# A fused linear-attention and feed-forward kernel: the opening's order of work written anew up to chunk 3, and the last tile stored in three pieces

## The chip, the core and the metric

The kernel runs on one core of a Trainium2 chip. The metric is the device time of one execution in microseconds (us). A core has a matrix engine (TensorE, PE in the profile, with its weight loads shown as PEld), a vector engine (VectorE, DVE), a scalar engine (ScalarE, ACT), a general engine (GpSimd, POOL) and a sync engine (SyncE, SP) that here only issues transfers. Transfers (DMAs) are done by 16 DMA engines that all queues share. Each engine works through its own list of instructions strictly in order; waits between engines are semaphores. TensorE reads SBUF, the on-chip memory, and writes PSUM, eight accumulator banks.

## What is computed

Lightning attention over 4 sequences (b) of 768 positions with 8 heads of 64 columns, and on its output a feed-forward block with an activation that has one slope per hidden column:

```python
for b in range(nb):                       # blocks of positions
    intra = (q_b @ k_b.T * Dmask) @ v_b
    inter = (q_b * lam_pow) @ kv_state
    out_b = intra + inter
    kv_state = lam_block * kv_state + (k_b * rev_pow).T @ v_b
x = out.transpose(0, 2, 1, 3).reshape(3072, 512)
h = x @ w_in                              # 512 -> 2048
g = maximum(h, 0) + alpha * minimum(h, 0)
y = g @ w_out                             # 2048 -> 512
```

q, k, v, w_in and w_out lie in DRAM as 32-bit floats, 4 MB for each of w_in and w_out; the matrix products are done in 16-bit floats.

## The kernel before, in words

The 3072 rows are cut into 6 chunks c of 512 rows. A chunk holds two sequences (bi = 0, 1) of 256 positions each, and each of these two groups of four heads (hh = 0, 1): four *units* per chunk, numbered n = 4c + 2bi + hh, 24 in all.

For a chunk's data, `load(c, bi, x, half)` (L80) issues from SP the transfer of k, q or v of one sequence: 512 KB, or with half 0 or 1 the 256 KB of one head group. There are five sets of buffers for these (L49). SP's transfers use eight semaphores in turn, so that a transfer also waits until the one issued eight before it has landed. `load_win(i)` and `load_wout(i)` (L95, L101) issue from POOL a quarter of w_in or w_out, which is cast to 16 bits on the way (1 MB read, 512 KB written). `gate(i, which)` (L109) is a transfer of a single element out of a weight quarter, issued from SP: since SP works in order, every load that stands behind it in SP's list waits until that quarter has landed.

A unit goes through these steps. `cast` (L254) makes 16-bit copies of k, q and v on ACT ("A"), DVE ("V") or POOL ("G"). `key_decayed` (L267) is the decayed k for the state. `transposes` (L284) brings q and k into columns, either on PE with a copy out of PSUM by ACT or DVE, or ("D") as a DMA transpose from SP; `transposed` (L310) does q or k alone on PE. `decayed` (L328) is the decayed q. `cluster(old, new)` (L343) is the matrix work: for `new` the scores s (L375) and the state update (L402), for `old` the state's part (L358) and the product of masked scores and v (L387); behind it the mask on DVE (L413), the copy of the old unit's output to XT on ACT or DVE (L420), and the state's copies R and RD (L433 to L451).

`up(c, f, bi, bank)` (L456) is one of 16 column blocks of h for a chunk (four matmuls of 512 columns, or of 256 with bi given, which needs just that sequence's two units), with the activation on ACT (L469) and DVE (L478). `down(c, t, part, 4, bank)` (L485) is a quarter of the sum for one of a chunk's four output tiles (four matmuls); part p reads quarter p of w_out, and up(f) reads quarter f // 4 of w_in. The last part calls `store` (L502): a copy on ACT and a transfer from SP. `down_last` (L509) does the output tiles of the last chunk, which nothing is left to overlap with; the last of them is cut into two halves of 256 columns. `fill` (L130) issues matmuls whose result nobody reads.

The order of all this is written out: the calls from L561 to L770 stand in the order in which each engine gets its instructions, and take the kernel to the end of up(1). From there, the loop at L772 weaves up(c) and down(c - 1) with the attention of chunk c + 1, for c = 2 to 5, and L781 ends with the last chunk's tiles. In that opening list, chunk 0's loads come first; the POOL list has load_win(0) and (1) at L611, (2) and (3) at L635, the four quarters of w_out at L639 and L657. SP's list has chunk 1's first sequence ungated (L620 to L625), gate(0, "out") ahead of the second sequence's k and q (L645), and gate(2, "out") ahead of chunk 2 (L688). Before up(0) gets going at L632 the list has 27 matmuls of `fill` behind the four of L146.

Of the kernel before, what the change touches and what calls it, by code (L numbers as in the profile page):

```python
# [11 lines left out]
def kernel(  # L12
# [102 lines left out]
    def zero_states(batches):  # L115
        for b in batches:
            for hh in (1, 0):
                nc.vector.memset(RD[b, hh], 0.0)
# [390 lines left out]
    def down_last(c, t, nc_parts):  # L509
        n = DM // nc_parts  # L510
        for x in range(nc_parts):
            o_ps = h_ps_pool.tile([128, DM], fp32, tag="h", name="o_ps")
            for f in range(NF):
                nc.tensor.matmul(  # L514
                    o_ps[:, 0:n],
                    lhsT=lhs(c, f, t),
                    rhs=w_out_sb[:, f, ts(x, n)],
                    start=(f == 0),
                    stop=(f == NF - 1),
                )  # L520
            store(c, t, o_ps, x * n, n)
# [38 lines left out]

    query_decay(2, 1)  # L561
    query_decay(1, 1)
    mask_logs(2)
    load(0, 0, "k", 0)
    query_decay(0, 1)
    cast(0, "k16", "G")
    load(0, 0, "q", 0)
    load(0, 0, "v", 0)
    load(0, 0, "k", 1)
    mask_logs(0)  # L570
    cast(0, "q16", "V")
    key_decay()
    load(0, 0, "q", 1)
    cast(0, "v16", "A")
    mask_logs(1)
    decay_mask(1)
    mask_logs(3)
    decay_mask(3)
    key_decayed(0, "G")
    load(0, 0, "v", 1)  # L580
    fill(4, "h")
    transposes(0, "V", False)
    decayed(0, "V")
    query_decay(3, 1)
    cast(1, "k16", "G")
    state_decay()
    cast(1, "q16", "G")
    load(0, 1, "k", 0)
    load(0, 1, "q", 0)
    load(0, 1, "v", 0)  # L590
    load(0, 1, "k", 1)
    load(0, 1, "q", 1)
    decay_mask(0)
    fill(5, "h")
    cluster(None, 0)
    slopes()
    transposed(1, 1, "V", "tk")
    cast(1, "v16", "A")
    transposed(1, 0, "A", "h")
    decayed(1, "P")  # L600
    fill(3, "op")
    cluster(0, None, "V")
    cast(2, "q16", "A")
    decay_mask(2)
    key_decayed(1, "G")
    key_decayed(2, "V")
    cast(2, "v16", "A")
    cast(2, "k16", "G")
    cluster(None, 1)
    transposed(2, 0, "V", "h")  # L610
    load_win(0)  # L611
    load_win(1)
    cast(3, "q16", "G")
    cast(3, "k16", "A")
    transposed(2, 1, "A", "op")
    query_decay(1, 0)
    fill(5, "tk")
    transposed(3, 1, "V", "tk")
    load(0, 1, "v", 1)
    load(1, 0, "k", None)  # L620
    transposed(3, 0, "A", "h")
    decayed(2, "G")
    cluster(1, 2, "A")
    load(1, 0, "q", None)
    load(1, 0, "v", None)  # L625
    cast(3, "v16", "A")
    key_decayed(3, "G")
    decayed(3, "G")
    fill(7, "h")
    cluster(2, 3, "A")  # L630
    fill(3, "op")
    up(0, 2, 0, "h")  # L632
    up(0, 0, 0, "h")
    cluster(3, None, "A")
    load_win(2)  # L635
    load_win(3)
    up(0, 1, 0, "h")
    up(0, 1, 1, "h")
    load_wout(0)  # L639
    load_wout(1)  # L640
    zero_states((2, 3))
    up(0, 3, None, "tk")
    up(0, 6, None, "h")
    key_decayed(5, "G")
    gate(0, "out")  # L645
    up(0, 7, None, "op")
    up(0, 0, 1, "h")
    load(1, 1, "k", None)
    up(0, 5, None, "tk")
    up(0, 2, 1, "h")  # L650
    up(0, 11, None, "op")
    load(1, 1, "q", None)
    up(0, 4, None, "h")
    up(0, 8, None, "tk")
    up(0, 10, None, "op")
    cast(4, "k16", "A")
    load_wout(2)  # L657
    load_wout(3)
    up(0, 15, None, "h")
    query_decay(2, 0)  # L660
    up(0, 9, None, "h")
    cast(5, "k16", "G")
    up(0, 12, None, "op")
    key_decayed(4, "V")
    up(0, 13, None, "tk")
    cast(5, "q16", "G")
# [146 lines left out]
```

## Time and profile before

| | us |
|---|---|
| three runs: median | 219.85 |
| three runs: lowest to highest | 219.68 to 221.3 |
| profiled execution: span from the first to the last instruction | 218.5 |
| the median over that span | 1.35 more |

No time but its span is given for the profiled execution itself. The span is taken by the hardware profiler and leaves out what lies around the first and last instruction. In the rows, "x4" is a count of instructions, the first two numbers of a row in order of time are its start and its length in us, and what stands in brackets is how long the engine had been idle and who ended that. L87 is a line of the kernel before. A busy PE isn't PE at its peak: matmuls overlap, and one of 512 columns that follows another adds 0.22 us while its own duration is shown as 0.38 us.

### The profile page before, as it was taken

The numbers are of one execution on the slowest core, as the hardware profiler recorded it, in microseconds if no ns is written. First come the engines' busy times: TensorE is split into PE (matmuls) and PEld (weight loads), VectorE is DVE, ScalarE is ACT, GpSimd is POOL, SyncE is SP. The second block draws the span as 40 slices with busy tenths as digits, with TensorE's granted clock in tenths as the row PEclk, the third lists the DMA queues.
The fourth block names the chain that finished last, engine by engine and source line by source line (L and its number), as shares of the span: only waits on it lengthen the run. The fifth ranks groups of instructions, "written<-read, shape, count | busy, mean of one in ns | idle before, by whom it ended". The sixth has DMA issues, their size and how long they took to land.

```text
span 218.5 us, 5177 instructions
## 1 busy us (share of the span) xinstructions
PE 206.5 (94%) x2065; PEld 104.7 (48%) x2065; DVE 131.5 (60%) x261; ACT 112.5 (51%) x216; POOL 92.3 (42%) x165
## 2 busy tenths in 40 slices
PE   7788899988979999999999999999999999999993
PEld 2454445544445444555545545554545444444453
DVE  7986788467879964866855646546645444444000
ACT  6886577246555575365456445545445434444121
POOL 4779300265099873697693484375331000000000
PEclk9999999999999999999999999999999999999999
DMA  5999999995799999689757997232111011110212
GB/s 149 297 274 215 216 214 206 270 282 153 184 273 208 315 238 209 164 208 231 176 126 192 149 244 222 57 96 65 35 51 48 0 51 49 48 48 0 99 48 96
DMA packets 62332, 33.90 MB, mean 155 GB/s; under 512 B 18132, under 2 KB 59364, under 8 KB 62308
## 3 DMA queue, kind: packets, MB, share of 16 engines
q1 hardware_dynamic: 58036, 29.37, 54.3%
q0 software_dynamic: 4224, 4.19, 11.4%
q8 instruction: 16, 0.26, 0.6%
q14 instruction: 8, 0.07, 0.1%
q10 hardware_dynamic: 48, 0.01, 0.0%
HBM read 27.27 MB, written 6.29 MB: 154 GB/s over the span
## 4 chain that ended last, share of the span: by engine, by line
PE 77%; DMA 11%; POOL 3%; DVE 3%; issue 2%; SPq 1%; ACT 1%; ACTq 0%; DVEq 0%
PE h_ps L461 34%; PE o_ps L491 29%; PE o_ps L514 6%; DMA w_in_sb<-in_moe_w_in_dram 6%; PE s L375 3%; DMA kraw<-in_k_dram 3%; DMA qkT<-qk 3%; PE acc L387 2%; PE acc L358 2%; SPq L87 1%; PE acc L402 1%; POOL RD L451 1%; DVE xT L243 1%; DVE sm L413 1%; POOL qdT L333 1%
## 5 line engine op out<-in xcount | busy, mean ns | idle before, releaser
L478 DVE SCALAR_TENSOR_TENSOR g<-m,oma,h_ps 128x512 f16<-128x512 f32 (+1 forms) x100 | 71.3, 724 | 57.3 <-ACT m L469 56.3
L461 PE MATMUL h_ps<-xT,w_in_sb 128*128 128x512 f16 (+1 forms) x400 | 95.0, 371 | 1.4 <-DMA w_in_sb<-in_moe_w_in_dram 1.3
L469 ACT ACTIVATE m<-h_ps 128x512 f32<-128x512 f32 (+1 forms) x100 | 57.7, 579 | 64.4 <-PE h_ps L461 62.3
L491 PE MATMUL o_ps<-w_out_sb,g 128*128 128x512 f16 x320 | 81.3, 379 | 0.0
L461 PEld LDWEIGHTS <-w_in_sb 128*128 128x128 f16 x400 | 38.1, 98 | 44.5 <-DMA w_in_sb<-in_moe_w_in_dram 2.7
L491 PEld LDWEIGHTS <-g 128*128 128x128 f16 x320 | 30.1, 98 | 34.1
L413 DVE TENSOR_TENSOR sm<-s,dmask 128x512 f16<-128x512 f32 x48 | 30.8, 684 | 7.5 <-PE s L375 7.0
L451 POOL COPY RD<-R 64x128 f16<-64x128 f16 x64 | 18.5, 289 | 36.2 <-DVE R L437 34.3
L333 POOL TENSOR_TENSOR qdT<-qkT,qdecay 128x512 f16<-128x512 f16 (+1 forms) x21 | 22.0, 1049 | 20.7 <-DVE qkT L243 17.0
L271 POOL TENSOR_TENSOR kdec<-kraw,kdecay 128x512 f16<-128x512 f32 x22 | 23.0, 1045 | 1.8 <-ACT kdecay L210 1.8
L504 ACT ACTIVATE o_sb<-o_ps 128x512 f32<-128x512 f32 (+1 forms) x25 | 14.5, 580 | 17.0 <-PE o_ps L514 11.1
L245 POOL CAST qk<-kraw 128x512 f16<-128x512 f32 x19 | 11.6, 610 | 11.3 <-DMA kraw<-in_k_dram 10.6
L437 DVE SCALAR_TENSOR_TENSOR R<-R,rdecay,acc 128x64 f16<-128x64 f16 x64 | 14.2, 274 | 3.0 <-ACT R L434 3.0
L241 ACT ACTIVATE xT<-acc 128x512 f16<-128x512 f32 x18 | 10.7, 597 | 8.7 <-PE acc L402 7.7
L514 PE MATMUL o_ps<-w_out_sb,g 128*128 128x512 f16 (+1 forms) x80 | 14.0, 336 | 0.0
L375 PE MATMUL s<-qkT 64*64 64x128 f16 x384 | 10.0, 222 | 1.8 <-DMA qkT<-qk 1.1
L514 PEld LDWEIGHTS <-g 128*128 128x128 f16 x80 | 7.8, 98 | 6.3
L358 PE MATMUL acc<-qdT,RD 128*128 128x128 f16 x80 | 8.4, 219 | 2.5 <-DVE R L437 1.1
L358 PEld LDWEIGHTS <-RD 128*128 128x128 f16 x80 | 6.0, 97 | 9.1 <-ACT R L434 2.0
L241 ACT ACTIVATE qk<-qraw 128x512 f16<-128x512 f32 x15 | 9.3, 622 | 0.7 <-DMA qraw<-in_q_dram 0.7
L387 PE MATMUL acc<-sm,v 64*64 64x128 f16 x384 | 9.6, 218 | 0.0
L375 PEld LDWEIGHTS <-qkT 64*64 64x64 f16 x384 | 6.2, 106 | 6.1 <-DMA qkT<-qk 2.0
(62 smaller groups left out, 108.6 us busy)
## 6 DMA issues: line engine op xcount, KB each, us to landing
out_dram<-o_sb SPq DMA_DIRECT2D x23, 256.0 KB, 2.0
kraw<-in_k_dram SPq DMA_DIRECT2D x10, 512.0 KB, 6.1
qraw<-in_q_dram SPq DMA_DIRECT2D x10, 512.0 KB, 6.0
vraw<-in_v_dram SPq DMA_DIRECT2D x10, 512.0 KB, 5.2
w_in_sb<-in_moe_w_in_dram POOLq DMA_DIRECT2D x4, 512.0 KB, 11.6
w_out_sb<-in_moe_w_out_dram POOLq DMA_DIRECT2D x4, 512.0 KB, 18.2
kraw<-in_k_dram SPq DMA_DIRECT2D x4, 256.0 KB, 5.6
qraw<-in_q_dram SPq DMA_DIRECT2D x4, 256.0 KB, 5.4
```

Source lines behind the costliest of these rows:

```text
L241: nc.scalar.activation(out, in_, AF.Copy)
L271: engine(eng).tensor_tensor(out=kdec, in0=kr, in1=kdecay[:, ds(4 * hh, 4), :].rearrange("p h e -> p e h").unsqueeze(3).to_broadcast([128, ...
L333: engine(eng).tensor_tensor(out=qdT[:, :, :, p], in0=(t["qps"] if eng == "P" else t["qkT"][:, 0])[:, :, :, p], in1=qdecay[:, hh, :, :, p], ...
L358: nc.tensor.matmul(ot[a][:, hp, :].rearrange("p (e j) -> p e j", e=2), lhsT=RD[bb, ho][:, a, hp].rearrange("p h d -> p (h d)"), rhs=to["qd ...
L375: nc.tensor.matmul(s[hl][ds(a * 64, 64), hp, 1 - e, :].rearrange("p (e j) -> p e j", e=2), lhsT=t["qkT"][p, 1, e, hp, ds(a * 64, 64)], rhs ...
L413: nc.vector.tensor_tensor(out=sm, in0=s[hl], in1=mask_of(hl, hh), op=ALU.mult)
L451: nc.gpsimd.tensor_copy(out=RD[b, hh][p, a, :, hl, :], in_=R[b, hh, 2 * pb + a][p])
L461: nc.tensor.matmul(h_ps[:, 0:n] if bi is None else h_ps[:, 0:n].rearrange("p (e j) -> p e j", e=2), lhsT=w_in_sb[:, gi, ts(f, 128)], rhs=x ...
L469: nc.scalar.activation(m[:, 0:n], h_ps[:, 0:n], AF.Relu, scale=-1.0)
L478: nc.vector.scalar_tensor_tensor(out=g, in0=mv, scalar=oma[:, f : f + 1], in1=hv, op0=ALU.mult, op1=ALU.add)
L491: nc.tensor.matmul(o_ps, lhsT=lhs(c, f, t), rhs=w_out_sb[:, f, :], start=(f == 0), stop=(f == NF - 1),)
L514: nc.tensor.matmul(o_ps[:, 0:n], lhsT=lhs(c, f, t), rhs=w_out_sb[:, f, ts(x, n)], start=(f == 0), stop=(f == NF - 1),)
```

## The change

The written-out list is replaced by another that goes on to the end of up(2); the loop starts at c = 3. As far as the next sections use it:

- q of both sequences of chunk 0, and v of the second, are loaded whole; the order is k (second head group first), q, v.
- POOL gets load_win(0), (1), (2), (3) and load_wout(2) with at most two casts or products between any two of them, and load_wout(0), (1) right behind decayed(3).
- SP gets gate(2, "out") after chunk 0 and two 256 KB pieces of chunk 1 (k and q of unit 4). All the rest of chunk 1, in pieces of 256 KB, stands behind this gate. gate(1, "out") stands ahead of the last two of them and of chunk 2. load_wout(3) stands in POOL's list behind key_decayed(7), which needs a piece of chunk 1 that is loaded behind the gate.
- Unit 8 is transposed on PE in place of a DMA; 15 DMA transposes are left of 16. `fill` has 35 matmuls in place of 27, 17 of them before the first transpose.
- Chunk 1's attention is mixed with down(0), chunk 2's with up(1) and down(1), most of chunk 3's with down(1) and up(2).
- zero_states(2) goes to POOL, written as integers.
- The last tile is stored as 256, 128 and 128 columns in place of 256 and 256.

```diff
-    def down_last(c, t, nc_parts):
-        n = DM // nc_parts
-        for x in range(nc_parts):
+    def down_last(c, t, widths):
+        x = 0
+        for n in widths:
...
-        down_last(NC - 1, t, 1 if t < 3 else 2)
+        down_last(NC - 1, t, (DM,) if t < 3 else (256, 128, 128))
```

The new list up to the point at which up(1) begins:

```diff
+    query_decay(2, 0)
     query_decay(2, 1)
+    load(0, 0, "k", 1)
+    load(0, 0, "k", 0)
+    load(0, 0, "q", None)
     query_decay(1, 1)
+    fill(11, "h")
+    load(0, 0, "v", 0)
+    mask_logs(0)
     mask_logs(2)
+    fill(6, "h")
+    load(0, 0, "v", 1)
+    key_decay()
+    key_decayed(0, "G")
+    mask_logs(3)
+    load(0, 1, "k", 0)
+    cast(1, "k16", "G")
+    cast(0, "v16", "G")
+    decay_mask(0)
+    cast(0, "k16", "V")
+    mask_logs(1)
+    cast(2, "k16", "G")
+    key_decayed(1, "G")
+    load_win(0)
+    load(0, 1, "q", None)
+    cast(0, "q16", "V")
+    state_decay()
+    transposed(0, 1, "V", "op")
+    load(0, 1, "k", 1)
+    decay_mask(2)
+    transposed(0, 0, "V", "h")
+    transposed(1, 1, "V", "op")
     query_decay(0, 1)
+    load(0, 1, "v", None)
     decay_mask(1)
+    key_decayed(2, "G")
+    load(1, 0, "k", 0)
     decay_mask(3)
+    load_win(1)
     query_decay(3, 1)
+    decayed(0, "P")
+    cast(1, "q16", "A")
+    load_win(2)
+    cluster(None, 0)
     fill(5, "h")
+    transposed(1, 0, "A", "h")
+    cast(1, "v16", "A")
+    cast(3, "q16", "G")
+    transposed(2, 1, "V", "h")
+    decayed(1, "P")
+    load_win(3)
+    cast(2, "q16", "V")
+    load_wout(2)
+    cluster(0, 1, "A")
+    transposed(2, 0, "A", "tk")
+    cast(2, "v16", "V")
+    decayed(2, "V")
+    cast(4, "k16", "V")
+    fill(8, "h")
+    load(1, 0, "q", 0)
+    cluster(1, 2, "A")
+    cast(3, "k16", "A")
+    fill(5, "op")
+    cast(3, "v16", "G")
+    cast(4, "q16", "G")
+    transposed(3, 0, "V", "tk")
+    key_decayed(3, "V")
+    transposed(3, 1, "A", "h")
+    gate(2, "out")
+    cluster(2, None, "A")
+    load(1, 1, "k", 1)
+    key_decayed(4, "G")
+    cluster(None, 3, "A")
+    decayed(3, "G")
     slopes()
+    transposes(4, "A", False)
+    up(0, 1, 0, "h")
+    up(0, 3, 0, "op")
+    cluster(3, None, "A")
+    up(0, 2, 0, "h")
+    load(1, 0, "v", 0)
+    up(0, 2, 1, "h")
+    decayed(4, "V")
+    load(1, 0, "q", 1)
+    load_wout(0)
+    up(0, 0, None, "op")
+    up(0, 7, None, "tk")
+    up(0, 5, None, "h")
+    load_wout(1)
...
+    up(0, 1, 1, "tk")
+    load(1, 1, "k", 0)
+    down(0, 0, 0, 4, "op")
+    down(0, 2, 0, 4, "h")
+    down(0, 2, 1, 4, "h")
+    key_decayed(7, "G")
+    load_wout(3)
+    load(1, 1, "v", 0)
+    zero_states((3,), "V")
+    load(2, 0, "k", 0)
+    cast(4, "v16", "G")
+    key_decayed(5, "G")
+    cast(7, "q16", "A")
+    load(2, 0, "q", 0)
+    down(0, 3, 0, 4, "h")
+    cast(6, "k16", "G")
+    cast(5, "q16", "V")
+    cast(5, "k16", "V")
+    down(0, 3, 1, 4, "h")
+    cluster(None, 4)
+    transposes(5, "A", False)
...
+    down(0, 0, 1, 4, "op")
+    decayed(5, "V")
...
+    down(0, 2, 2, 4, "h")
...
+    cluster(4, 5, "A")
+    transposes(7, "A", False)
...
+    down(0, 0, 2, 4, "op")
+    cast(6, "q16", "A")
+    down(0, 3, 2, 4, "h")
+    cluster(5, 7, "A")
+    down(0, 0, 3, 4, "op")
...
+    transposes(6, "A", False)
...
+    cluster(7, 6, "A")
+    transposes(8, "A", False)
+    down(0, 1, 0, 4, "h")
...
+    down(0, 1, 1, 4, "h")
+    cluster(6, 8, "A")
...
+    down(0, 1, 2, 4, "h")
+    up(1, 4, None, "op")
...
+    cluster(15, 16, "A")
+    cast(17, "v16", "G")
+    up(2, 12, None, "tk")
+    cast(18, "v16", "G")
+    key_decayed(18, "G")
 
-    for c in range(2, NC):
+    for c in range(3, NC):
```

More of the change, by code (lines that the diff above doesn't have):

```diff
@@ L615 @@
-    transposed(2, 1, "A", "op")
-    query_decay(1, 0)
[L617 to L657, printed above, removed]
```

312 lines of the change are left out of this document (165 added, 147 removed).

## The prediction

> **What bounds the kernel now.** I read the page's busy shares first, then the busy time of each engine by stage, cut where the work changes.
>
> ```profile
> PE 206.5 (94%) x2065; PEld 104.7 (48%) x2065; DVE 131.5 (60%) x261; ACT 112.5 (51%) x216; POOL 92.3 (42%) x165
> ```
> ```profile
> 24.24:44.25 20.01, 20.01 (x142) 9.96 (x146) 14.15 (x24) 11.36 (x24) 2.32 (x4) 1.00 1.20 230
> 44.25:63.47 19.22, 16.09 (x296) 8.63 (x296) 14.28 (x33) 10.43 (x24) 9.22 (x13) 1.00 0.87 217
> 63.47:110.49 47.02, 46.84 (x556) 24.14 (x557) 36.36 (x76) 26.23 (x46) 34.75 (x65) 1.00 0.94 218
> 110.49:201.36 90.87, 90.87 (x714) 44.27 (x713) 47.23 (x77) 43.19 (x73) 29.02 (x55) 1.00 0.35 88
> ```
> Columns are stage, length, then busy us of PE, PEld, DVE, ACT, POOL, the granted clock, DMA share and GB/s. From 63 us on PE has practically no idle time, at full clock. 110.49 is where up(3, 0) starts, the first call that both versions' loop has in common (read by counting the steps in PE's order). From there on both lists are the same up to the last tile, and PE is full: 108.0 us of the span that the change can't shorten, save in the last tile. What is open is when up(3, 0) starts.
>
> How far that is from the least, I get by pricing PE's work in the full stretch. The chain of work gives the unit price.
>
> ```profile
> 37.49 0.45 PE tp L299 x8
> ...
> 41.55 2.59 PE o_ps L491 x12
> ...
> 57.17 5.71 DMA qkT<-qk
> ```
> Four matmuls of an up or a down cost 2.59/3 = 0.864 us. The stretch 110.49:201.36 holds ups and downs of three chunks, 96 x 0.864 = 82.9; the other 8.0 us are about eight clusters, so 1.0 us each (estimate; 0.88 for chunk 0 and 1, whose state part is half as large). A PE transpose of a unit costs 0.45.
>
> ```profile
> 20.02 1.05 PE L461 MATMUL h_ps<-xT,w_in_sb 128*128 128x256 f16 x8 [0.54 <-DMA w_in_sb<-in_moe_w_in_dram]
> ...
> 24.24 2.98 PE L461 MATMUL h_ps<-xT,w_in_sb 128*128 128x512 f16 x15 [0.73 <-DMA w_in_sb<-in_moe_w_in_dram]
> ```
> The first up starts at 20.02. From there to up(3, 0) PE must do 48 ups and 32 downs (80 x 0.864 = 69.1), clusters for units 4 to 7 (3.5), 8 to 15 (8.0) and the halves of 3 and 16 (0.9), and four PE transposes (1.8): 83.3 us. It takes 90.5. So about 7.1 us are stalls, 1.1 of them before 24.24 (4.22 us that hold three ups and a half cluster). That is the prize. Where they are, PE's rows show:
>
> ```profile
> 48.07 0.27 PE L358 MATMUL acc<-qdT,RD 128*128 128x128 f16 x2 [0.48 <-ACT qk L241]
> ...
> 52.47 0.27 PE L358 MATMUL acc<-qdT,RD 128*128 128x128 f16 x2 [0.85 <-DVE R L437]
> ...
> 62.92 0.42 PE L375 MATMUL s<-qkT 64*64 64x128 f16 x16 [1.12 <-DMA qkT<-qk]
> ```
> Clusters of chunk 1 stand too close together between 44 and 56, so each waits for mask, state and transpose copies of the one before; at 62.92 the wait is for unit 8's DMA transpose, 5.71 us in the chain. Each visible wait also refills PE's pipeline (0.16 us overlap lost).
>
> **The transfers.** Two kinds share the 16 engines: SP's (hardware) and POOL's weights (software).
>
> ```profile
> q1 hardware_dynamic: 1610, 0.80, 115.2%
> ```
> ```profile
> q0 software_dynamic: 2025, 2.01, 84.7%
> q1 hardware_dynamic: 1936, 0.98, 34.2%
> ```
> ```profile
> q0 software_dynamic: 1243, 1.23, 123.7%
> q1 hardware_dynamic: 3, 0.00, 0.1%
> ```
> These are the queues in 11.7:14.5, 16:30 and 32:38 (packets, MB, share). Alone, SP's go at 0.80/2.8 = 290 GB/s, 0.9 us for 256 KB. Alone, weights go at 205 GB/s of what they write, 2.56 us a quarter. Together they take 144 and 70: 3.7 us a quarter and 3.7 us for 256 KB. A quarter that goes alone is 1.1 us sooner, a load beside it four times slower.
>
> ```profile
> 34.14 0.74 SPq L113 DMA_DIRECT2D gates<-w_out_sb  x1
> 34.93 0.38 SPq L87 DMA_DIRECT2D kraw<-in_k_dram  x1
> 35.35 0.57 SPq L87 DMA_DIRECT2D qraw<-in_q_dram  x1
> ```
> ```profile
> q0 software_dynamic: 703, 0.70, 123.3%
> q1 hardware_dynamic: 2, 0.00, 0.1%
> ```
> The second fence is 35:38.4: three loads are issued and nothing of them moves for 3.5 us, since weights stand ahead. The other way round, 11.7:14.5 moves no weights though two quarters were issued from 10.77 on:
>
> ```profile
> 3.82 0.61 POOL L245 CAST qk<-kraw 128x512 f16<-128x512 f32 x1 [1.11 <-DMA kraw<-in_k_dram]
> 6.26 1.05 POOL L271 TENSOR_TENSOR kdec<-kraw,kdecay 128x512 f16<-128x512 f32 x1 [1.82 <-ACT kdecay L210]
> ...
> 10.21 0.61 POOL L245 CAST qk<-kraw 128x512 f16<-128x512 f32 x1 [0.17 <-DMA kraw<-in_k_dram]
> 10.77 1.68 POOL L96 DMA_DIRECT2D w_in_sb<-in_moe_w_in_dram  x2
> ```
> So a kind waits for what the other had queued (on the other side of that stretch the first quarter lands 9.2 us after its issue, below). [...]
>
> **The change, step by step.** Prices are rows of this trace.
>
> ```profile
> L413 DVE TENSOR_TENSOR sm<-s,dmask 128x512 f16<-128x512 f32 x18 | 11.6, 685 | 6.1 <-PE s L375 5.8 <-ACT dmask L204 0.3
> ...
> L271 POOL TENSOR_TENSOR kdec<-kraw,kdecay 128x512 f16<-128x512 f32 x8 | 8.4, 1048 | 1.8 <-ACT kdecay L210 1.8
> ...
> L241 ACT ACTIVATE qk<-kraw 128x512 f16<-128x512 f32 x4 | 2.5, 626 | 2.3 <-DMA kraw<-in_k_dram 2.3
> ...
> L433 ACT ACTIVATE RD<-acc 64x128 f16<-64x128 f32 x16 | 4.3, 267 | 7.2 <-DVE xT L243 4.6 <-PE acc L402 2.5
> ...
> L434 ACT ACTIVATE R<-acc 128x128 f16<-128x128 f32 x8 | 2.2, 277 | 0.2
> ...
> L241 ACT ACTIVATE qkT<-tp 128x1024 f16<-128x1024 f16 x1 | 1.0, 1018 | 0.0
> ```
> ```profile
> w_in_sb<-in_moe_w_in_dram POOLq DMA_DIRECT2D x1, 512.0 KB, 9.2
> ```
> ```profile
> qraw<-in_q_dram SPq DMA_DIRECT2D x1, 512.0 KB, 14.4
> ```
> ```profile
> w_out_sb<-in_moe_w_out_dram POOLq DMA_DIRECT2D x4, 512.0 KB, 18.2
> ```
> These tell us from issue to landing: the w_in quarter of 10.77, the q of unit 4 and 5 of 11.02, and w_out's median.
>
> *Start of up(0).* Chunk 0's loads land at 3.8 and then every 0.9 us: k of sequence 1's first group, the seventh 256 KB, at 10.2 as now; q whole at 12.0, v whole at 14.8. POOL: key_decayed(0) to 7.3 as now, two casts to 9.05, cast(2) 10.3 to 10.9, key_decayed(1) to 11.95, so load_win(0) is issued at 11.95 against 10.77. Its first bytes go at about 15.3, when SP's 14 pieces are through, and it lands at 19.7 (now 19.97), because no load is beside it. cluster(1, 2) waits for cast(2, "v16") on DVE (v at 14.8) until 15.2, cluster(None, 3) for DVE's two masks, R, copy and key_decayed(3) until 19.3. transposes(4), then the first up at 20.1. No gain: the price is chain length, and it could as well be 19.6 or 21.5. The extra `fill` matmuls stand where PE would idle (0.22 each once warm; the 17 first end near 7.9, when k and q of unit 0 are cast). Then two ups and the half cluster, and a wait of 0.4 for XT of unit 3 at 22.6, against 1.1 of stalls now.
>
> *The weights in a row.* At 2.6 us each w_in's quarters land at 19.7, 22.3, 24.9, 27.5, first used at 20.1, 23.6, 26.1, 27.9. Only the last is close: 0 to 1 us of stall, I take 0.2. w_out(2) lands at 30.0, (0) 32.6, (1) 35.2; down(0, 0, 0) needs (0) at 34.8, down(0, 2, 1) needs (1) at 36.5. No stall, by 1.3 us.
>
> *The gate.* SP stands still from about 16 to 30.0, with nothing behind it but chunk 1, chunk 2 and stores. Eight pieces are issued from 30.7 on; they move when w_out(1) is through (33.7), then land every 0.9 us: (1,1)k1 at 36.0, v of unit 4 at 36.9, q and k of unit 5 at 37.8 and 38.7, q of unit 7 at 39.6, v of units 5 and 7 at 40.5 and 41.4, q of unit 6 at 42.3. Before, q of units 4 and 5 is there at 11.02 + 14.4 = 25.4 and the loads for 6 and 7 are issued from 34.93 on; so the cover of units 4 and 5 goes, and 6 and 7 gain. PE reaches cluster(None, 4) at 39.1, transposes(5) at 39.6 (needs 39.3): no stall, margin 0.3. Then ACT is the narrow one: it holds cast(7, "q16") (0.63) in line until 39.6, then the state's copies, a transpose copy of 1.0 and cast(5, "v16") follow, so cluster(4, 5) waits 0.5, transposes(7) 0.4, cluster(5, 7) 0.6, cluster(6, 8) 0.4: 1.9.
>
> *w_out(3) behind key_decayed(7).* Issued at 37.1, behind SP's backlog, lands at 46.5; down(0, 0, 3) wants it at 46.7. Behind it in SP's list the rest of chunk 1 shares with it: k and v of unit 6 at 46.0 and 47.0, used at 47.6 and 49.8. 0 to 2 us; I take 0.
>
> *Unit 8 on PE*: 0.45 added, and the 1.12 wait at 62.92 is gone with the rest of the 7.1. *Chunk 2 and 3 spread over up(1), down(1), up(2)*: at least four ups or downs between clusters, 3.5 us, against a cluster's follow-up of two masks (2 x 0.685) on DVE, and the output copy and state copies (0.6 + 2 x 0.267 + 0.277) on ACT. POOL's list (products of 1.05 to 1.16) runs 3 to 9 us ahead of PE there. 0; without that cover each of eight clusters could wait 0.5. *zero_states(2)* on POOL: two memsets in a POOL that waits anyway, 0.
>
> *The last tile.* After PE ends, ACT copies and SP stores.
>
> ```profile
> 211.81 0.60 ACT L504 ACTIVATE o_sb<-o_ps 128x512 f32<-128x512 f32 x1 [2.91 <-PE o_ps L514]
> 213.55 0.38 ACT L504 ACTIVATE o_sb<-o_ps 128x256 f32<-128x256 f32 x1 [1.15 <-PE o_ps L514]
> 215.30 0.38 ACT L504 ACTIVATE o_sb<-o_ps 128x256 f32<-128x256 f32 x1 [1.36 <-PE o_ps L514]
> ```
> The slope from 512 to 256 columns makes a copy of 128 columns 0.1 shorter; the transfer is no longer. 32 matmuls of 128 columns take PE what 16 of 256 did (1.75 us from copy to copy) if their weight loads hide; L358, 128 columns with as many weight loads, is no slower in its rows above (0.27 for two). Bounds: +0.8 if half of the loads don't hide, -0.2; I take -0.1.
>
> *Sum.* Stalls removed 7.1. Added before up(3, 0): start 0.1, XT 0.4, last w_in 0.2, chunk 1's copies 1.9, unit 8 0.45: 3.05. It starts at 110.49 - 4.05 = 106.4; with -0.1 at the last tile the span is 218.5 - 4.15 = 214.35. The median of before is 1.35 over the span; with the same, 215.7 us.
>
> **The rivals.** A measurement of this kernel tells 1%, 2.2 us, from no change.
>
> 1. *Chunk 1 comes 3 us later than laid out.* Place: ACT's cast(7, "q16"), DVE's cast(5, "q16"), PE's transposes(5). The gate opens when a transfer issued fifth lands; margin there is 0.3 us, beyond it each us costs one. Median landing of w_out is 18.2 us now, so 3 us is not much. 215.7 + 3 = 218.7, no change. For it: chunk 1's first sequence loses its early load. Against: fewer bytes are ahead of the gate.
> 2. *Slower: w_out(3) shares with chunk 1.* If key_decayed(7) gets its piece early and the weights start at once, the pieces of 36 to 42 take 3.7 us each, not 0.9. Three of them (v of unit 5 and 7, q of unit 6) make 8 us, less margins of 1.2: 215.7 + 6.8 = 222.5. It turns the sign once more than 4.15 are lost. Against: the two 3 us delays above.
> 3. *No new stalls.* All but unit 8's 0.45 comes back: 219.85 - 6.65 = 213.2. Against: the ACT copies are counted from rows.
> [...]
>
> **How the numbers follow.** Forecast 0.50 (214.3 to 217), rival 4 0.10, rival 3 0.07, rival 1 0.21, rival 2 0.12. Faster by over 1% (below 217.65): 0.50 + 0.10 + 0.07 = 0.67; within 1% 0.21; slower 0.12. The range, 213.2 to 219.8, holds the forecast, 3, 4 and most of 1, and leaves rival 2 and a little of 1 out.
>
> **What would show it.** First up at 19.6 to 21; no SP issue between 17 and 29, gate ending near 30 (now 34.14); up's from 23 to 35 without a gap over 0.3 us; transposes(5) near 39.6; up(1, 4) near 55; up(3, 0) at 106 to 107; from there to the end 107.9. I am wrong if PE's rows show waits over 1 us for loads behind the gate, if w_out(3) lands after 48, or if clusters after 56 wait for POOL.

## The result and the profile after

| | before | after |
|---|---|---|
| median of four runs beside each other, us | 220.22 | 216.71 |
| lowest to highest | 219.68 to 221.3 | 216.34 to 217.79 |
| after / before, 95% interval | | 0.9844 [0.9806, 0.9881] |
| spans of the four runs of after | | 216.0, 214.7, 214.6, 215.1 |

The change makes the kernel 1.6% faster; 215.7 was forecast, within 213.2 to 219.8. The profiled execution of after is the slowest of its four, so that its opening, read below, is worse than a usual one. Every run takes 1.8 us more than its span; the 1.35 of the forecast was the distance between a median and the span of another execution.

The page of after has:

```profile
PE 207.9 (96%) x2097; PEld 107.7 (50%) x2097; DVE 138.2 (64%) x274; ACT 114.3 (53%) x218; POOL 85.5 (40%) x153
```

The busy time of each engine by stage, cut at the first up, the halves of chunk 1, up(3, 0) and the last tile:

```profile
23.12:45.00 21.88, 21.88 (x171) 11.76 (x168) 16.97 (x35) 14.54 (x32) 4.37 (x7) 1.00 1.18 243
45.00:56.87 11.87, 11.87 (x257) 7.44 (x255) 8.65 (x20) 10.15 (x23) 4.19 (x6) 1.00 0.98 260
56.87:107.60 50.73, 50.73 (x606) 26.16 (x605) 44.93 (x94) 28.88 (x50) 32.27 (x57) 1.00 0.99 210
107.60:198.50 90.90, 90.90 (x714) 44.31 (x713) 48.55 (x81) 43.20 (x73) 29.25 (x55) 1.00 0.33 86
198.50:216.00 17.50, 13.86 (x96) 7.92 (x94) 0.52 (x1) 3.33 (x7) 0.00 (x0) 1.00 0.20 75
```

In each of the first four rows PE's busy time is the whole stage. The 3.1 us that PE stood idle in 44.25:63.47 of before are gone, and the stage from up(3, 0) to the last tile is as long as before (90.90 against 90.87). So the kernel can be told in three lengths: the start of the first up, from there to the last tile, and the end.

```profile
23.12 1.04 PE L464 MATMUL h_ps<-xT,w_in_sb 128*128 128x256 f16 x8
```
```profile
198.47 13.91 PE o_ps L517 x96
```

| | first up at | to the last tile | the end | span |
|---|---|---|---|---|
| before | 20.02 | 181.34 | 17.1 | 218.5 |
| forecast | 20.1 | 177.2 | 17.0 | 214.35 |
| after, as profiled | 23.12 | 175.35 | 17.5 | 216.0 |

The middle gained 6.0 us and the opening lost 3.1 of them, the end 0.4. Why the opening lost is in the rows in order of time (line, operation, what ended the idle time):

```profile
12.06 1.95 DVE L246 CAST qk<-qraw 128x512 f16<-128x512 f32 x1
12.65 1.06 POOL L274 TENSOR_TENSOR kdec<-kraw,kdecay 128x512 f16<-128x512 f32 x1
14.06 0.40 PE L322 MATMUL tpx<-ident,qk 128*128 128x128 f16 x4 [1.49 <-DVE qk L246]
14.30 3.40 PE L140 MATMUL unread<-ident 128*128 128x512 f16 x8
```

and in windows of 1 us, where the number after POOL's is PE's granted clock:

```profile
14.00:15.00 1.00, 0.94 (x7) 0.54 (x8) 1.00 (x3) 0.50 (x1) 1.00 (x2) 0.76 1.24 266
15.00:16.00 1.00, 1.00 (x4) 0.37 (x3) 1.00 (x4) 0.10 (x1) 1.00 (x3) 0.50 1.21 211
16.00:17.00 1.00, 1.00 (x3) 0.29 (x2) 0.77 (x3) 0.00 (x0) 1.00 (x2) 0.50 1.23 205
17.00:18.00 1.00, 1.00 (x12) 0.46 (x14) 0.00 (x0) 0.00 (x0) 1.00 (x3) 0.53 1.24 207
```

DVE's cast of unit 2's q takes 1.95 us while POOL issues a weight quarter and then multiplies. For DVE's casts of q the same profile has, shortest, median and longest in ns:

```profile
L246 DVE CAST qk<-qraw x6: 361/419/1945, 7.2 to 90.3; 128x512 f16<-128x512 f32 x6
```

PE idles 1.49 us; and then the granted clock is one half for 0.48 + 1 + 1 + 0.94 = 3.4 us. In that time the eight matmuls of `fill(8, "h")`, which nothing reads, stand in PE's line and take 3.40 us; in a_kdec_later, with the clock at 1.00, the same eight take 1.89.

The transfers came as laid out. The gate ends at 30.08, and the eight loads go out behind it:

```profile
29.34 0.74 SPq L113 DMA_DIRECT2D gates<-w_out_sb  x1
30.13 0.39 SPq L87 DMA_DIRECT2D kraw<-in_k_dram  x1
```

w_in's quarters land at 19.15, 21.75, 24.26 and 26.84 (forecast 19.7 to 27.5), w_out(2), (0) and (1) at 29.32, 31.91 and 34.64 (30.0, 32.6, 35.2), w_out(3) at 44.00 (46.5), and the five of chunk 1's first loads whose landing the trace has at 36.28, 38.02, 38.96, 39.80 and 40.65 (36.9, 38.7, 39.6, 40.5 and 41.4 forecast).

### The profile page after: what moved, and what is told of

It reads as the page before. It is cut to its first block, busy times and chain, and to the rows that moved or that the text cites. A ratio compares the mean times of both kernels' runs of the same rounds, so it can differ in the third digit from the quotient of the medians.

```text
span 216.0 us, 5257 instructions
## 1 busy us (share of the span) xinstructions
PE 207.9 (96%) x2097; PEld 107.7 (50%) x2097; DVE 138.2 (64%) x274; ACT 114.3 (53%) x218; POOL 85.5 (40%) x153
## 4 chain that ended last, share of the span: by engine, by line
PE 91%; DMA 3%; DVE 2%; ACT 1%; issue 1%; SPq 0%; ACTq 0%; DVEq 0%
PE h_ps L464 39%; PE o_ps L494 33%; PE o_ps L517 6%; PE s L378 4%; DMA qraw<-in_q_dram 3%; PE acc L390 2%; PE acc L361 2%; PE unread L140 1%; PE acc L405 1%; DVE qk L246 1%; PE tp L302 1%; PE tpx L322 1%; SPq L87 0%; DVE qkT L246 0%; DVE sm L416 0%
## 5 line engine op out<-in xcount | busy, mean ns | idle before, releaser
L464 PE MATMUL h_ps<-xT,w_in_sb 128*128 128x512 f16 (+1 forms) x400 | 92.8, 371 | 0.0
L454 POOL COPY RD<-R 64x128 f16<-64x128 f16 x64 | 21.3, 333 | 42.2 <-DVE R L440 40.4
L274 POOL TENSOR_TENSOR kdec<-kraw,kdecay 128x512 f16<-128x512 f32 x19 | 19.8, 1048 | 15.5 <-DMA kraw<-in_k_dram 11.7
L507 ACT ACTIVATE o_sb<-o_ps 128x512 f32<-128x512 f32 (+2 forms) x26 | 14.6, 565 | 21.2 <-PE o_ps L517 10.9
L244 ACT ACTIVATE xT<-acc 128x512 f16<-128x512 f32 x22 | 13.2, 598 | 13.7 <-PE acc L405 12.0
L336 POOL TENSOR_TENSOR qdT<-qkT,qdecay 128x512 f16<-128x512 f16 (+1 forms) x14 | 16.1, 1148 | 1.8 <-DVE qkT L246 1.6
L517 PE MATMUL o_ps<-w_out_sb,g 128*128 128x512 f16 (+2 forms) x96 | 14.1, 308 | 0.0
L248 POOL CAST qk<-kraw 128x512 f16<-128x512 f32 x15 | 9.6, 637 | 11.2 <-DMA kraw<-in_k_dram 10.5
L140 PE MATMUL unread<-ident 128*128 128x512 f16 x35 | 10.3, 448 | 0.0
L248 POOL CAST v<-vraw 128x512 f16<-128x512 f32 x13 | 8.4, 650 | 0.7 <-DMA vraw<-in_v_dram 0.7
```

The lines of the kernel that those rows point to most:

```text
L248: nc.gpsimd.tensor_copy(out=out, in_=in_)
L274: engine(eng).tensor_tensor(out=kdec, in0=kr, in1=kdecay[:, ds(4 * hh, 4), :].rearrange("p h e -> p e h").unsqueeze(3).to_broadcast([128, ...
L336: engine(eng).tensor_tensor(out=qdT[:, :, :, p], in0=(t["qps"] if eng == "P" else t["qkT"][:, 0])[:, :, :, p], in1=qdecay[:, hh, :, :, p], ...
L454: nc.gpsimd.tensor_copy(out=RD[b, hh][p, a, :, hl, :], in_=R[b, hh, 2 * pb + a][p])
L464: nc.tensor.matmul(h_ps[:, 0:n] if bi is None else h_ps[:, 0:n].rearrange("p (e j) -> p e j", e=2), lhsT=w_in_sb[:, gi, ts(f, 128)], rhs=x ...
L517: nc.tensor.matmul(o_ps[:, 0:n], lhsT=lhs(c, f, t), rhs=w_out_sb[:, f, ds(x, n)], start=(f == 0), stop=(f == NF - 1),)
```

## The experiments

All ratios are to the kernel before, run on the same chip. The table has the three lengths of each profiled execution. A run without an interval was executed once.

| run | ratio, 95% interval | first up | to the last tile | span |
|---|---|---|---|---|
| after | 0.9844 [0.9806, 0.9881] | 23.12 | 175.35 | 216.0 |
| a_cast_act | 0.9857 [0.9821, 0.9893] | 21.43 | 175.59 | 214.5 |
| a_kdec_later | 0.9809 [0.9774, 0.9844] | 21.52 | 175.34 | 214.4 |
| a_no_fill8 | 0.9838 [0.981, 0.9865] | 21.72 | 175.34 | 214.6 |
| c_dec2p | 0.9811 [0.9771, 0.9851] | 21.38 | 175.47 | 214.4 |
| a_port | 0.9825 [0.9792, 0.9859] | 20.79 | 177.11 | 215.6 |
| a_tail256 | 216.41 us | 21.25 | 175.53 | 214.6 |
| a_no_gate2 | 1.0006 [0.9979, 1.0033] | 21.62 | 180.23 | 219.4 |
| a_dense | 223.41 us | 21.73 | 182.37 | 221.6 |
| a_unit8_dma | 1.0333 [1.0275, 1.0391] | 21.68 | 186.44 | 225.6 |
| b_unit8_pe | 1.0136 [1.0086, 1.0187] | 19.89 | 184.10 | 221.2 |
| b_tail128 | 219.87 us | 19.66 | 181.61 | 218.1 |

### What the gate is worth

After without its new first gate:

```diff
     transposed(3, 1, "A", "h")
-    gate(2, "out")
     cluster(2, None, "A")
```

> The changed kernel without gate(2, out): chunk 1's pieces are no longer held and go beside the weights from 17 us on. If the row of weights is what matters, as I forecast: a quarter takes 3.7 us in place of 2.6 while it has company, w_in's last lands at 29 to 31 (26.8 in the changed kernel), w_out(0) and (1) at 35 to 40 (31.9, 34.6), PE waits 0.5 to 3 us in all for weights between 25 and 42, and the span is 0.5 to 3 longer than its start alone would give. Rival, the late start left the row with slack of 2 to 3 us, so the gate is worth nothing: no wait over 0.2 us, span 214.3 to 216.2 according to the start.

Measured: 221.02 us, ratio 1.0006 [0.9979, 1.0033]: all that the change had gained is gone. PE's rows with waits over 0.3 us between 23 and 45:

```profile
28.34 1.90 PE L464 MATMUL h_ps<-xT,w_in_sb 128*128 128x512 f16 x8 [0.52 <-DMA w_in_sb<-in_moe_w_in_dram]
31.99 7.10 PE L464 MATMUL h_ps<-xT,w_in_sb 128*128 128x512 f16 x40 [1.75 <-DMA w_in_sb<-in_moe_w_in_dram]
...
42.93 2.75 PE L494 MATMUL o_ps<-w_out_sb,g 128*128 128x512 f16 x12 [1.75 <-DMA w_out_sb<-in_moe_w_out_dram]
```

The queues in 16:28 of this run, and then of after (packets, MB, share of 16 engines):

```profile
q0 software_dynamic: 1689, 1.68, 82.8%
q1 hardware_dynamic: 1770, 0.88, 35.9%
```
```profile
q0 software_dynamic: 2453, 2.44, 123.0%
q1 hardware_dynamic: 9, 0.00, 0.2%
```

In the same 12 us the weights move 2.44 MB alone and 1.68 beside chunk 1's loads. Each quarter lands 3.65 us after the one before instead of 2.6 (w_in at 21.0, 24.64, 28.29, 31.94), and PE waits 4.0 us in the three rows. From the first up to the last tile 4.9 us are lost. The loss has the place that my theory gave it and is larger than the 0.5 to 3 us that I allowed for. In this order the whole gain hangs on the gate; what the row of weights would do in the order of before, no run tells.

### What the spacing of chunk 1's clusters is worth

After with seven downs moved from between chunk 1's clusters to behind the last of them:

```diff
     transposes(7, "A", False)
...
-    down(0, 0, 2, 4, "op")
...
-    down(0, 3, 2, 4, "h")
     cluster(5, 7, "A")
-    down(0, 0, 3, 4, "op")
...
     transposes(6, "A", False)
...
-    down(0, 2, 3, 4, "h")
...
-    down(0, 3, 3, 4, "h")
...
     cluster(7, 6, "A")
     transposes(8, "A", False)
-    down(0, 1, 0, 4, "h")
...
-    down(0, 1, 1, 4, "h")
     cluster(6, 8, "A")
+    down(0, 0, 2, 4, "op")
+    down(0, 3, 2, 4, "h")
+    down(0, 0, 3, 4, "op")
+    down(0, 2, 3, 4, "h")
+    down(0, 3, 3, 4, "h")
+    down(0, 1, 0, 4, "h")
+    down(0, 1, 1, 4, "h")
```

> The changed kernel with seven of the downs that stand between chunk 1's clusters moved behind cluster(6, 8): the clusters of units 5, 7, 6 and 8 follow each other with transposes alone between them, as far as PE goes. The work is the same. Theory (spacing is what took the stalls of the kernel before away): each of these clusters waits for the masks, state copies and transpose copy of the one ahead, 1.5 to 2.5 us each, so up(1, 4) starts 4 to 8 us later after the first up than in the changed kernel (33.75 us after it there), and the span is 218 to 223. Rival (the stalls of the kernel before came from late loads of chunk 1): the waits sum to less than 2 us.

Measured: span 221.6, 7.0 us more from the first up to the last tile than in after. PE's waits:

```profile
46.51 0.27 PE L361 MATMUL acc<-qdT,RD 128*128 128x128 f16 x2 [1.48 <-DVE R L440]
49.64 0.27 PE L361 MATMUL acc<-qdT,RD 128*128 128x128 f16 x2 [1.49 <-DVE R L440]
51.34 0.62 PE L302 MATMUL tp<-ident,qk 128*128 128x128 f16 x8 [0.62 <-DVE qk L246]
53.01 0.27 PE L361 MATMUL acc<-qdT,RD 128*128 128x128 f16 x2 [1.05 <-DVE R L440]
```
```profile
54.00:57.00 3.00, 3.00 (x8) 1.08 (x8) 1.72 (x6) 0.60 (x1) 1.12 (x3) 0.51 1.13 289
```

The waits are of the kind that before had at 48.07 and 52.47, for the state and for a cast, 4.6 us together. So the rival, less than 2 us, is out, though each wait is 0.6 to 1.5 us where my theory had 1.5 to 2.5. Behind them the clock is at one half (0.51 in the second fence, windows of 54 to 57, and 0.76 in the next us), so that the downs which were moved there take longer too. My theory did not have that; at half of some 3.4 us it is 1.7 of the 7.0 (an estimate). In after the same four clusters and eight downs fill 44.88 to 56.87 without an idle row.

### Unit 8 on PE: each half alone

The transposes of unit 8 on PE in the order of before, and by DMA in the order of after:

```diff
-    transposes(8, "D", False)
+    transposes(8, "A", False)
```
```diff
-    transposes(8, "A", False)
+    transposes(8, "D", False)
```

> The kernel before with unit 8's transposes on PE in place of the DMA transpose, nothing else. I had put 1.12 us of its 7.1 us of stalls on that wait, and 0.45 on the transposes. If that is so, the wait at cluster(None, 8) is gone, the span is 0.5 to 0.8 shorter (217.7 to 218.0) and the time 0.2 to 0.4% less. Rival: another wait (decayed(8) on POOL, or the masks of cluster(6, None)) takes its place, span 218.3 to 219.2.

> The after kernel with unit 8 transposed by a DMA as before, at the same place of the list (transposes(8, "D")). My step put the PE transpose at +0.45 of PE's time and the end of the 1.12 us wait for the DMA. Theory: in the new order the DMA's 5.7 us from the cast of unit 8 on are hidden by the eight ups and downs that now stand ahead of cluster(7, 8) or they are not by less than 1 us; span 213.9 to 215.2, no difference that a measurement tells. Rival: the DMA's transpose waits behind weights and loads of chunk 2, its cluster waits 1 us or more as before: span 215.3 to 216.5, a wait <-DMA qkT at the cluster's s matmuls.

Measured: both are slower than before itself, by 1.4% and 3.3%. The PE rows in question, first of b_unit8_pe, then of a_unit8_dma:

```profile
52.97 0.80 PE L299 MATMUL tp<-ident,qk 128*128 128x128 f16 x8 [3.40 <-ACT qk L241]
```
```profile
62.94 0.64 PE L378 MATMUL s<-qkT 64*64 64x128 f16 x16 [9.12 <-DMA qkT<-qk]
```

and SP's list in a_unit8_dma, with a row of the windows (clock 0.50 again):

```profile
53.21 2.24 SPq L510 DMA_DIRECT2D out_dram<-o_sb  x1
55.56 0.37 SPq L87 DMA_DIRECT2D vraw<-in_v_dram  x1
56.02 1.40 SPq L510 DMA_DIRECT2D out_dram<-o_sb  x1
57.60 2.13 SPq L292 DMA_TRANSPOSE qkT<-qk  x1
```
```profile
58.00:62.00 4.00, 0.00 (x0) 0.00 (x0) 0.00 (x0) 0.00 (x0) 0.00 (x0) 0.50 1.20 250
```

On PE in the old order, the transpose stands in PE's list ahead of work that is ready, and holds it 3.4 us until ACT, through with the copies of the cluster before, casts unit 8's k. By DMA in the new order, unit 8's k and q are cast by 51.2, but SP reaches the transpose only at 57.60, behind loads and stores of its own list, and it takes 5.3 us more: PE waits 9.12. Neither expectation of b_unit8_pe was met; in a_unit8_dma the rival has the kind of the wait right and a ninth of its size. The part that I had priced at 0.45 us of work against 1.12 of waiting decides over 11.1 us in the new order (186.44 - 175.35): SP's list runs late there, and a transpose in that list is late with it. That the gate is what makes the list late is argued from its rows; no run has this transpose without the gate.

The 1.12 us that I had priced weren't unit 8's. The order of before has these rows, of SP and of PE:

```profile
53.69 2.07 SPq L289 DMA_TRANSPOSE qkT<-qk  x1
57.17 2.92 SPq L289 DMA_TRANSPOSE qkT<-qk  x1
```
```profile
57.12 0.42 PE L375 MATMUL s<-qkT 64*64 64x128 f16 x16
```

Counted in PE's order, the cluster at 57.12 is cluster(None, 8). Unit 8's transpose was issued at 53.69, right behind its casts, landed at 57.1, and the row shows no wait. The wait at 62.92 is that of cluster(None, 9), for unit 9's transpose, issued at 57.17. So b_unit8_pe took away a transfer for which PE hardly waited, and put a wait of 3.40 us in its place.

### The opening

Four kernels take away what stood together at 12 us in after: the cast goes to ACT; POOL's product goes behind the next two weight quarters; the eight fills are left out; and a product reads PSUM.

```diff
-    cast(2, "q16", "V")
+    cast(2, "q16", "A")
```


> The changed kernel with one edit: the 16-bit copy of unit 2's q is made by ACT in place of DVE. Theory 1 (a blocked copy, then a cold TensorE): in the changed kernel this copy takes 1.95 us on DVE (0.42 elsewhere) because POOL's key_decayed(2) runs from 12.65 to 13.71; PE idles 1.49 us behind it, and then runs at a granted clock of 0.50 from 14.5 to 17.9, so that 8 fill matmuls take 3.4 us in place of 1.7. With the copy on ACT (0.62) PE's gap there is under 0.5 us, the granted clock is 1.00 after 5 us, the first up starts at 20.0 to 20.8 (23.1 in the changed kernel), the span is 213.0 to 213.9 (216.0) and the ratio to the kernel before 0.970 to 0.976. Theory 2 (chunk 0's whole loads of q and v set the start): the first up stays at 22.5 or later and the span within 0.6 of 216.0.

```diff
-    key_decayed(2, "G")
...
     decayed(0, "P")
...
     load_win(2)
+    key_decayed(2, "G")
```


> The changed kernel with one edit: POOL does key_decayed(2) behind load_win(2), not ahead of load_win(1); the copy of unit 2's q stays on DVE. Theory 1, with POOL's product as what blocks the copy: at 12.06 POOL issues weight transfers, the copy takes 0.42 to 1.0 us, PE's gap falls below 0.7, the clock stays at 1.00, the first up starts at 20.0 to 21.2, span 213.2 to 214.5. If POOL's issuing of weight transfers blocks the copy as its product does, the copy takes 1.5 us or more (issuing goes on until about 14.2) and the first up stays at 22.5 or later. Theory 2 (late loads): first up at 22.5 or later, too, with a copy of 0.42 that starts late.

```diff
-    fill(8, "h")
```


> The changed kernel without the 8 fill matmuls that stand behind unit 2's transpose. They take 3.4 us at half clock, and PE does nothing else meanwhile. Theory 1a (these 8 are the delay): cluster(1, 2) starts at 15.3 to 16.3 in place of 17.5, the first up at 21 to 22, span 214 to 215. Theory 1b (they also bring the clock back): without them PE is idle again, the granted clock stays at 0.5 beyond 17.9, by at least one more stretch of 3.4 us, and the first up comes hardly earlier (22 to 23.5) or the first ups run at half clock; span 215 to 217.5. Theory 2 (late loads): cluster(1, 2) can't start before v at 16.1, first up at 21.5 to 22.5.

On top of a_kdec_later:

```diff
-    decayed(2, "V")
+    decayed(2, "P")
```


> The after kernel with key_decayed(2, "G") six steps later (as in the run a_kdec_later, ratio 0.9809, span 214.4) and with decayed(2, "P"): unit 2's product with the decay reads the transposed q from PSUM, not its copy in SBUF. Theory (DVE and POOL hold each other up when both work on SBUF): the operation falls from 1.30 us to about 0.41, as the other units' products from PSUM do, the masks of cluster(1, 2) and all behind it come up to 0.9 sooner, the first up starts at 20.4 to 21.0 instead of 21.5, span 213.5 to 214.2. Rival (the first up is set by chunk 0's last load of v, landing at 14.9, and by DVE's sum of work, or what is gained is waited for again at w_in's quarters and the gate): first up at 21.3 to 21.6, or earlier with waits of the same size at the ups behind it; span 214.3 to 214.8.

Measured: first ups at 21.43, 21.52, 21.72 and 21.38; medians of 216.78, 216.14, 216.59 and 216.07 us, and ratios whose intervals all overlap with that of after. Against after's opening as it usually goes, this is no gain: a_tail256, a_unit8_dma and a_dense have the same list up to the first up, and start it at 21.25, 21.68 and 21.73. The clock is 1.00 in a_tail256's windows from 11 to 17, and in a_dense the stretch at 54 to 58 makes up all that its mean of 0.992 lacks. With the cast on ACT the idle time falls from 1.49 to 0.29 us and the clock stays up in the profiled execution (1.00 in its windows from 11 to 17). In three of the six runs the mean clock is 0.992 all the same, which is what 3.4 us at one half make of the span, and these are the longest (217.16 to 218.62 us, the others 216.28 to 216.39): this cast is not all that brings the clock down. With POOL's product moved away the cast takes 0.81 in place of 1.95, and PE idles 0.34; in a_tail256, where the product stays and the cast starts 0.8 later, it takes 0.89. Without the fills the cast is again slow (1.75) and the clock falls (0.69 and 0.60 in the windows below), but the eight matmuls no longer stand in PE's line meanwhile:

```profile
12.06 1.75 DVE L246 CAST qk<-qraw 128x512 f16<-128x512 f32 x1
...
13.86 0.40 PE L322 MATMUL tpx<-ident,qk 128*128 128x128 f16 x4 [1.27 <-DVE qk L246]
```
```profile
15.00:16.00 1.00, 0.47 (x10) 0.31 (x14) 1.00 (x5) 0.00 (x0) 1.00 (x2) 0.69 1.16 203
...
18.00:19.00 1.00, 1.00 (x5) 0.33 (x4) 0.47 (x2) 0.99 (x3) 1.00 (x2) 0.60 1.23 206
```

Theory 1a is right here: 21.72 at half clock without the fills lies within what the list with them takes at full clock (21.25 in a_tail256, 21.73 in a_dense), while half clock and fills together cost 1.4 to 1.9 us (23.12). Theory 2, late loads, is out: the first ups are ahead of 22.5, and without the fills cluster(1, 2) starts at 15.53. None of the four comes to the 20.1 of the forecast, nor a_cast_act and a_kdec_later to the first ups that theory 1 gave them, since steps behind the cast take longer in turn. In a_cast_act:

```profile
15.30 1.30 DVE L336 TENSOR_TENSOR qdT<-qkT,qdecay 128x256 f16<-128x256 f16 x1
15.69 0.62 POOL L248 CAST qk<-qraw 128x512 f16<-128x512 f32 x1
...
19.06 1.44 DVE L274 TENSOR_TENSOR kdec<-kraw,kdecay 128x512 f16<-128x512 f32 x1
```

In a_no_fill8 the first takes 0.41 and the second 0.68; POOL only issues transfers as the first starts there, and is idle as the second starts. c_dec2p was to tell whether reading PSUM makes the first short. It can't: in a_kdec_later, on which it is built, the same operation reads SBUF and takes 0.41 already, as it does in after, a_no_fill8 and a_tail256; the 1.30 that I set out from is a_cast_act's.

```profile
15.97 0.41 DVE L336 TENSOR_TENSOR qdT<-qkT,qdecay 128x256 f16<-128x256 f16 x1
```

The rows of c_dec2p:

```profile
11.57 2.42 POOL L96 DMA_DIRECT2D w_in_sb<-in_moe_w_in_dram  x3
...
12.21 1.29 DVE L246 CAST qk<-qraw 128x512 f16<-128x512 f32 x1
...
15.84 0.41 DVE L336 TENSOR_TENSOR qdT<-tpx,qdecay 128x256 f16<-128x256 f16 x1
16.17 0.41 DVE L246 CAST qk<-kraw 128x512 f16<-128x512 f32 x1
```

Its transpose of unit 2 starts 0.14 us earlier than in a_kdec_later, and its first up the same 0.14; the edit between the two adds nothing. In both the last wait before the first up is for key_decayed(3) on DVE, which takes 1.83 beside POOL's cast and products. In a_tail256 it takes 0.83, and PE's longest wait from 10 us on is for ACT's cast of unit 3's k:

```profile
18.72 0.40 PE L322 MATMUL tpx<-ident,qk 128*128 128x128 f16 x4 [0.55 <-ACT qk L244]
```

Several chains end within some tenths of each other, and no single one of these steps holds the first up. A fifth kernel, a_port, moves unit 4's share of this work behind the first ups as well:

```diff
-    cast(2, "q16", "V")
+    cast(2, "q16", "A")
...
-    cast(4, "q16", "G")
...
-    key_decayed(4, "G")
...
-    transposes(4, "A", False)
...
-    decayed(4, "V")
...
     load_wout(1)
+    cast(4, "q16", "G")
+    key_decayed(4, "G")
...
     up(0, 12, None, "op")
+    transposes(4, "A", False)
+    decayed(4, "V")
```

> The changed kernel with the copy of unit 2's q on ACT, and with unit 4's copy of q, decayed k (both POOL), transposes and decayed q moved from before the first up to behind it (POOL: behind load_wout(1); PE and DVE: behind up(0, 12)). In the run with the copy alone the first up still started at 21.4, behind DVE's key_decayed(3), which took 1.44 us beside POOL's work on unit 4 (0.68 in the kernel before). Theory 1, DVE and POOL hold each other up when both read SBUF: key_decayed(3) takes 0.7 on DVE, the first up starts at 20.0 to 20.6 and the span is 213.1 to 213.8 (214.5 with the copy alone); the ratio to the kernel before 0.970 to 0.978. Rival, the start is a chain of its own and DVE's length beside POOL doesn't matter: first up at 21.2 to 21.6, less the 0.45 of the transposes at most. Second rival, the gained start is lost behind the gate, since chunk 1's pieces land by 36 to 41 whatever PE does: waits of 0.5 us or more between 36 and 45, span 214.0 to 214.5.

Measured: 217.02 us, ratio 0.9825 [0.9792, 0.9859]. The operation does what theory 1 says of it, and this run is the one that shows it: with POOL's work on unit 4 moved away, key_decayed(3) takes 0.67 us in place of 1.44. That reading SBUF is what the two share there is not shown.

```profile
19.16 0.67 DVE L274 TENSOR_TENSOR kdec<-kraw,kdecay 128x512 f16<-128x512 f32 x1
```

The first up starts at 20.79, above theory 1's 20.0 to 20.6 and where the rival has it (21.2 to 21.6 less 0.45): it comes 0.64 earlier than in a_cast_act, and up to 0.45 of that are the transposes that were moved. The middle is 1.8 us longer:

```profile
22.25 0.27 PE L361 MATMUL acc<-qdT,RD 128*128 128x128 f16 x2 [0.42 <-ACT m L472]
34.93 0.61 PE L302 MATMUL tp<-ident,qk 128*128 128x128 f16 x8 [0.61 <-DVE g L481]
```

These waits and the 0.45 make 1.5 of it, so the work put off is paid for later; they don't stand between 36 and 45, where the second rival had them. I found no order that beats after by more than the interval; a_kdec_later and c_dec2p (0.981) are the best, 0.3% below after's 0.984, which these runs don't separate.

### The last tile

After with its last tile in two pieces, and before with it in three:

```diff
-        down_last(NC - 1, t, (DM,) if t < 3 else (256, 128, 128))
+        down_last(NC - 1, t, (DM,) if t < 3 else (256, 256))
```
```diff
-        down_last(NC - 1, t, 1 if t < 3 else 2)
+        down_last(NC - 1, t, (DM,) if t < 3 else (256, 128, 128))
```

> The changed kernel with the last tile in two halves of 256 columns again. From the first matmul of the last tiles to the end it took 17.50 us with 256, 128, 128 columns and 17.14 in the kernel before with 256 and 256, where I had forecast 0.1 less. If the three pieces are what costs, this stretch is 17.1 to 17.2 here; if it is the length of the last transfer, which varies by itself, it is 17.3 to 17.6.

> The before kernel with its last tile in 256, 128 and 128 columns. It settles whether the third piece itself costs something at the end. The span from the end of the last ACT copy to the end was 2.83 in before (two pieces of 256), 3.22 to 3.25 in after (256, 128, 128), 3.51 in after with two pieces of 256. Theory A (the end behind the last store is longer in the new kernel whatever the pieces, by some 0.7): here 2.4 to 2.6, span about 0.3 to 0.4 shorter than before's. Theory B (it comes from the pieces): 3.2, and no gain.

Measured, from the start of the last tiles to the end of the span:

| | 256, 256 | 256, 128, 128 |
|---|---|---|
| order of before | 17.1 | 16.8 |
| order of after | 17.8 | 17.5 |

The third piece is worth 0.3 us in both, by one execution of each; the eight other kernels with three pieces in the order of after have 17.5 to 17.7, so this is not far from the spread. The 17.8 is neither value of a_tail256's expectation. PE's time of these tiles is the same (13.87 and 13.91). The end of after is 0.7 longer than that of before with either: all of it lies behind the last copy, whose end is 2.6 us before the end of the span in b_tail128 and 3.3 in after, and even behind the last bytes stored: the DMA engines move nothing in the last 1.4 us of before and the last 2.0 of after. Theory A holds. What in the new kernel lengthens its end stays open; no run here takes it apart.

## Why the prediction was right, point by point

**What bounds the kernel: right.** From up(3, 0) on the time is that of before, and what could be won was PE's idle time ahead of it. Its size, 7.1, is borne out too: from the first up to the last tile 6.0 us are won, and 0.45 of work was added.

**Start of up(0): mis-sized.** I said 20.1, "as well 19.6 or 21.5". It was 23.12 in the profile and 21.25 to 21.7 in the other runs with after's opening: 1.2 us at the least. I priced each DVE step by a row in which POOL was idle or only issued transfers. The rows of before had the other price too: the first decayed q takes 0.75 us on DVE at 7.63, beside a cast on POOL, where the same product took 0.41 in a_kdec_later; but I never asked what POOL did meanwhile. Here casts of 0.42 take 0.8 to 1.95 and products of 0.41 and 0.68 take up to 1.30 and 1.83. For one product a_port shows that POOL's work is the cause; that such delays make up the 1.2 us is argued, since the last waits before the first up differ from run to run, and in after's own opening they are ACT's as well, which my chain did not have. The rest, up to 23.12, is the clock, which no sum of mine had: one half for 3.4 us. The same kernel does not meet it in every run: after's four have mean clocks of 0.992, 1.0, 0.997 and 1.0. The clock fell behind 1.49 us of idle time in one piece, while a_no_gate2, with a mean of 0.997, runs at full pace behind a piece of 1.75 (12 matmuls in 2.75 us, 0.22 each and 0.16 for the last one's end). So the length of the idle piece alone doesn't decide.

**The 0.4 for XT, 0.2 for the last w_in and 1.9 for chunk 1's copies: too much.** Together with unit 8's 0.45 PE had 83.75 us of work from the first up to up(3, 0), by my prices; it took 107.60 - 23.12 = 84.48. So 0.7 were lost where I had 2.5, and no row of PE shows a wait. PE came to transposes(5) 3.1 us and to up(1, 4) 1.9 us later than I laid it out while the transfers came up to 0.8 earlier, so that the waits for data had that much more room; and for the copies I took every operation of ACT's list as if in front of its cluster. With first ups at 21.25 to 21.7 the length is the same to 0.25 us. At 20.79 it isn't (a_port), though there other work was moved too. So part of this gain may be the other side of the late start; that is argued, not shown.

**The weights in a row and the gate: right.** Landings agree to 0.8 us but for w_out(3), which came 2.5 earlier; the step is worth 4.9 us against the same order without the gate, 4.2 of them waits of PE for weights (the three rows and one of 0.20).

**Chunk 1's spacing: right,** and worth 7.0 us against the same order without it. The values of the parts are not a sum: without either one the whole gain is gone.

**Unit 8 on PE: right in sign, wrong in what I compared it with.** The price of 0.45 holds, but I set it against before's wait of 1.12 at 62.92, which is for unit 9's transpose; unit 8's had landed before PE needed it. In the new order the alternative costs 11.1, which my list didn't have. That the step came out well is luck as far as my reason for it goes. What ended unit 9's wait in the new order, no run takes apart.

**The last tile: -0.1 was -0.3,** and +0.7 behind the last copy came from nowhere in my list.

**The sum.** The forecast had a span of 214.35 and 1.35 around it; the four runs have 214.6 to 216.0 and 1.8. With a start of 21.25, a middle of 175.5 and an end of 17.5 a run would take 214.3: errors of +1.2, -1.7 and +0.5 cancel. So that 215.7 lies near 216.71 is partly luck. The size of the stalls isn't, and neither are the gate and the spacing, the two steps that were to remove them.

**The rivals.** Rival 1 did not happen: chunk 1's loads came on time, and PE reached transposes(5) at 42.7, not 39.6. Rival 2 did not: w_out(3) was issued at 36.55 and landed at 44.00, and chunk 1's pieces up to 40.65 kept 0.9 us apart. Rival 3's middle (nothing but unit 8's 0.45 given back) is close to what happened, with the late start on top. Rival 4, weights beside chunk 0's last loads from 12 us on (0.10 of the chances), is shown by no run: the queues in 12:15 of after, where POOL had issued its first quarter at 11.71,

```profile
q1 hardware_dynamic: 1503, 0.75, 100.1%
q0 software_dynamic: 82, 0.08, 16.7%
```

show that SP's loads kept nearly all of the engines in these 3 us: 82 packets of weights moved, where weights alone (2453 in 12 us, above) would move some 610.

## What to carry to other kernels

Before a chain of short DVE steps is priced, look at what POOL does beside each of them: here casts of 0.42 us took up to 1.95, and one product took 1.44 us with POOL's work beside it and 0.67 with that work moved away. Loads that are wanted later are worth holding back behind the weights that are wanted now (a quarter landed every 2.6 us alone and every 3.65 beside loads), but then look at what else in that queue's list comes late, and take out of it what is wanted early: here the kernel with unit 8's transpose on PE and without the gate gained nothing (1.0006), and the one with the gate and that transpose by DMA lost 3% (1.0333). And matmuls whose result nobody reads should not stand ahead of work on the path: eight of them took 1.89 us at a clock of 1.00 and 3.40 at one half.

## What was not expected of the hardware

- A cast on DVE was long beside POOL's issuing of transfers alone, but not every one: in c_dec2p one takes 1.29 us while POOL does nothing but issue three quarters, and the next but one takes 0.41 beside a later issue. What decides isn't shown.
- The granted clock fell to one half for 3.4 us behind 1.49 us of idle PE in after, and with two pieces of 1.27 us in a_no_fill8 (0.69 in 15:16). It stayed at 1.00 behind pieces of 1.48 and 1.49 in a_dense (it fell there only behind the next two, of 0.62 and 1.05), and PE ran at full pace behind two of 1.75 in a_no_gate2. What decides isn't shown.
- The time from the last copy to the end of the span is 0.7 us longer in one kernel than in the other, with the same pieces stored: 3.3 in after, 2.6 in b_tail128.
